# Loads, ones, masks and visits: four rearrangements in a fused attention and SwiGLU kernel on one core

## The chip, the cores and the metric

One core of a Trainium2 chip runs the whole kernel. The metric is device time in microseconds (us), the median of several executions of one build. Each execution also has its span (what the profile covers, some 1.7 to 1.9 us shorter) and the mean clock that the throttle granted TensorE. An execution that is over 1.5% above the fastest of the same kernel is called slow. Verdicts use the others and a threshold of 2%.

## The reference

Attention with ALiBi-like slopes over 8 global keys and the last 96 keys, then a feed-forward block. There are 4 batches, 8 heads, 768 positions and head size 64.

```python
rel = pos[:, None] - pos[None, :]
is_global = pos[None, :] < 8
is_local = (rel >= 0) & (rel < 96)
keep = is_global | is_local
dist = np.where(is_global & ~is_local, 96.0, np.abs(rel))
scores = q @ k.T / 8 - slopes * dist          # -1e9 where not keep, then softmax
x = (softmax @ v)                             # (3072, 512)
xn = x / sqrt(mean(x*x) + 1e-6) * rms_g
g = xn @ w_gate                               # 512 x 1536
out = (g * sigmoid(g) * (xn @ w_val)) @ w_out # 1536 x 512
```

## The kernel before

The positions are cut into 8 *units* of 384 (half a batch). A list scheduler with estimated durations puts every operation on an engine, in an order that is fixed when the kernel is built. Attention of a unit makes scores (`sc`), exps (`P`), a product with a table (`TB`, the exp of the bias with zeros for the mask), values (`avp`) and a norm; then *feed* `fc` does the feed-forward of one unit. TensorE is meant to be busy all the time: attention of later units is slipped between the matmuls of a feed. Unit 0 and feed 0 have nothing to slip into. Feed 0 runs in two parts, of one block and of two blocks of 128 positions ("part 1" below is the second).

The parts that matter here (cuts marked `...`):

```python
# the first block of unit 0: f32 by the SP queue, cast, small transposes
def load_first(name, g):
    nc.sync.dma_start(both[ds(64 * g, 64), "qk".index(name)], ...)
def cast_first(name, eng): ...            # both -> first, bf16
def tr_first(g):                          # 8 transposes of 64x64, twice
    ...
# the column of ones beside V, which gives the softmax's sum
def ones(i):
    nc.vector.memset(V1[i][:, :, :, 64:65], 1.0)
...
ones_ops = [add("DVE", 0.1, 0.15, 5.0 + 10 * i, ones, i) for i in range(2)]

# a visit to the scores: one head pair p, diagonal (d=0) or off-diagonal (d=1) blocks
def qk(c, p, d):
    sc = [bank([128, 512], F32, tag="sc", ...) for hh in range(2)]
    for i in range(HB):                   # HB = 3 blocks of 128
        ...
            nc.tensor.matmul(sc[hh][:, ts(i, 128)], k_of(...)[r], q_of(c, p, i)[r], ...)
def ex(c, p, d, hh):                      # exp of up to 384 columns
    nc.scalar.activation(T["P", c, p, d][:, hh, lo:HB, :], ...)
def mask(c, p, d, eng): ...
em = "POOL" if c == 1 and not d else "DVE"     # unit 1's diagonal masks on GpSimd
def table_copy():
    nc.gpsimd.tensor_copy(TB[:, :, 2], TB[:, :, 1])
# the small copy of the global keys that an off-diagonal visit of units 0 and 1 needs: kg, 128x16
# an order that matters later: every load waits for the one eight before it
more["deps"] = list(more.get("deps", ())) + loads[-8:-7]
```

The softmax here doesn't subtract the row's maximum and nothing guards it: scores larger than these inputs give would overflow.

Of the kernel before, what the change touches and what calls it, by code (L numbers as in the profile page):

```python
# [13 lines left out]
F32 = mybir.dt.float32  # L14
# [128 lines left out]
def kernel(  # L143
# [59 lines left out]
    both = mp.tile([128, 2, 4, 2 * D], F32, tag="h", name="both", bufs=2)  # L203

    def load_first(name, g):
        nc.sync.dma_start(both[ds(64 * g, 64), "qk".index(name)],
                          (q if name == "q" else k)[0, ds(4 * g, 4), 0:128].rearrange("h (p i) d -> p h (i d)", i=2))

# [15 lines left out]
    for g in range(2):  # L224
        for name in "qk":
            load_first(name, g)
# [28 lines left out]
    nc.vector.memset(VG[0][:, :, :, 64:65], 1.0)  # L255
    ts_, stt = nc.vector.tensor_scalar, nc.vector.scalar_tensor_tensor
# [35 lines left out]
    def ones(i):  # L292
        nc.vector.memset(V1[i][:, :, :, 64:65], 1.0)

    def table_copy():
        nc.gpsimd.tensor_copy(TB[:, :, 2], TB[:, :, 1])
# [28 lines left out]
    def cast_first(name, eng):  # L325
        if "first" not in T:
            T["first"] = mp.tile([128, 2, 2, 4, D], BF16, tag="t", name="first", bufs=3)
        n = "qk".index(name)
        (nc.scalar.copy if eng == "ACT" else nc.vector.tensor_copy)(
            T["first"][:, n].rearrange("p i h d -> p h i d"), both[:, n].rearrange("p h (i d) -> p h i d", i=2))  # L330

    def tr_first(g):
        t = bank([128, 2, 2, 128], BF16, tag="v", name="trf", bufs=2)
        r = slice(64 * g, 64 * g + 64)
        for n in range(2):
            for x in range(2):
                for i in range(2):
                    nc.tensor.transpose(t[:, n, x, ds(64 * i, 64)], T["first"][r, n, i, ds(2 * x, 2), :], ident[r, r])
        T["trf", g] = t

# [9 lines left out]

    def cp_first(g, name, eng):
        copy = nc.scalar.copy if eng == "ACT" else nc.vector.tensor_copy
        d = qT_tile(0)[:, 0, ds(2 * g, 2)] if name == "q" else slots(0)[:, 0, ds(2 * g, 2), 0:128]
        copy(d.rearrange("p h (t i) -> p h t i", i=2),
             T["trf", g][:, "qk".index(name)].rearrange("p h (i t) -> p h t i", i=2))
# [24 lines left out]
    def ex_block(i, d, hh):  # L380
        t = ptp.tile([128, 2, HB, 128], BF16, tag=f"P{hh}", name=f"P{hh}", bufs=4)
        T["Pb", i, d, hh] = t.rearrange("p h i t -> p (h i) t")[:, 0:HP]
        nc.scalar.activation(T["Pb", i, d, hh], T["sb", i, d][hh], AF.Exp, scale=float(scale))
# [145 lines left out]
    def qk(c, p, d):  # L529
        half = c % 2  # L530
        sc = [bank([128, 512], F32, tag="sc", name=f"sc{hh}", bufs=2) for hh in range(2)]
        for i in range(HB):
            J = HB * half + i - d
            if J < 0:
                continue
            cu, j = (c, i - d) if i - d >= 0 else (c - 1, HB - 1)
            for hh in range(2):
                r = slice(64 * hh, 64 * hh + 64)
                nc.tensor.matmul(sc[hh][:, ts(i, 128)], k_of(cu, p, j, NG * d)[r], q_of(c, p, i)[r],  # L539
                                 start=True, stop=True)  # L540
        T["sc", c, p, d] = sc

    def ex(c, p, d, hh):
        lo = 1 if (c % 2 == 0 and d) else 0
        if ("P", c, p, d) not in T:
            T["P", c, p, d] = ptp.tile([128, 2, HB, 128], BF16, tag=f"P{d}", name=f"P{d}", bufs=4)
        nc.scalar.activation(T["P", c, p, d][:, hh, lo:HB, :],  # L547
                             T["sc", c, p, d][hh][:, ds(128 * lo, CH - 128 * lo)], AF.Exp,
                             scale=float(scale))

    def mask(c, p, d, eng):
        half = c % 2
        mul = (nc.vector if eng == "DVE" else nc.gpsimd).tensor_tensor
        P = T["P", c, p, d]
        if d == 0:
            m = TB[:, ds(2 * p, 2), 0:HB] if half == 0 else _brd(TB[:, ds(2 * p, 2), 1], 2, HB)
            mul(P, P, m, op=ALU.mult)  # L557
        else:
            lo = 1 if half == 0 else 0
            mul(P[:, :, lo:HB, :], P[:, :, lo:HB, :], _brd(TB[:, ds(2 * p, 2), 3], 2, HB - lo), op=ALU.mult)  # L560

# [3 lines left out]
    def av(c, p):  # L565
        b, half = divmod(c, 2)
        P0, P1 = T["P", c, p, 0], T["P", c, p, 1]
        o = bank([128, HB, 2, 65], F32, tag=av_tag(c, p), name="avp", bufs=1)
        for i in range(HB):
            I = HB * half + i  # L570
            for hh in range(2):
                h = 2 * p + hh
                nc.tensor.matmul(o[:, i, hh, :], P0[:, hh, i, :], V1[b % 2][:, I, h, :],  # L573
                                 start=True, stop=(I == 0))
                if I > 0:
                    nc.tensor.matmul(o[:, i, hh, :], P1[:, hh, i, :], VG[b % 2][:, I - 1, h, :],  # L576
                                     start=False, stop=True)
# [45 lines left out]
    def xt_tile(fc):  # L623
        if ("xT", fc) not in T:
            T["xT", fc] = xp.tile([128, 4, CC, 128], BF16, tag="xT", name="xT", bufs=3)
# [53 lines left out]
    def fh(fc, f):  # L679
        n = 128 * FCH[fc][1]  # L680
        if ("h", fc) not in T:
            T["h", fc] = mp.tile([128, FC, 512], BF16, tag="h", name="hb", bufs=2)
# [25 lines left out]
    def fh0(lo, n, f0):  # L708
        if ("h", 0) not in T:
            T["h", 0] = mp.tile([128, FC, 512], BF16, tag="h", name="hb", bufs=2)  # L710
# [4 lines left out]
    OP = 3  # L715

# [32 lines left out]
    def store(fc, j):  # L749
# [3 lines left out]
        sizes=dict(g=2, v=2, o=1, sc=2, av=1, P0=4, P1=4, u=2, t=3, h=2, xT=3, xu=2, xn=2, ob=3,  # L753
# [33 lines left out]
    class _Landed:  # L787
        eng, dma, start = "SP", ("hw", 0.0), 0.0

        def __init__(self, t):  # L790
            self.done = t

    landed = {("q", 0): _Landed(4.2), ("k", 0): _Landed(4.5), ("q", 1): _Landed(4.8), ("k", 1): _Landed(5.2)}
    plan.sw = 3.0
    plan.rings["h"].append(_Buf("h", 0))
    plan.rings["t"].append(first_t := _Buf("t", 1))
# [30 lines left out]
    stage_buf = {c: {n: buf(n + "b", (HB - 1, HP, 1)[min(c, 2)]) for n in "qk"} for c in range(NU)}  # L827
# [5 lines left out]
    def attention0():  # L833
        ld, v_ops = loaded[0]
        for n, i, x in (("k", 1, 0), ("q", 1, 0), ("v", 0, 1), ("k", 2, 0), ("q", 2, 0), ("v", 1, 1), ("v", 2, 1)):
            if x:
                v_ops.append(load(load_v, (0, i, 1), 2.0, 0.84))
            else:
                ld[n, i] = load(load_qk, (0, n, i), 2.0, 0.84, take=[stage_buf[0][n]] if i == 1 else [])
        qT_buf[0], kT_buf[0] = buf("qT", 5), buf("kT", 5 + HP)  # L840
        cast = {n: add(e, *x, 4.0, cast_first, n, e, deps=[landed[n, 1]])
                for n, e, x in (("q", "DVE", (0.53, 0.6)), ("k", "ACT", act(512)))}
        ready = {}
        def copies(o, t, key, fn, n, due):
            ready[key] = []
            for name, e in (("q", "ACT"), ("k", "DVE")):
                take = [] if key != ("f", 0) else [qT_buf[0] if name == "q" else kT_buf[0]]
                ready[key].append(add(e, *(act(n) if e == "ACT" else dve(n)), due, fn, key[1], name, e, deps=[o],
                                      give=[t], take=take, after=ready["f", 0][-1:] if key != ("f", 0) and name == "k" else ()))
        for g in range(2):  # L850
            t = buf("v", 2)
            o = add("PE", 0.5, 0.75, 5.0, tr_first, g, deps=list(cast.values()), take=[t],
                    give=[first_t] if g else [])
            copies(o, t, ("f", g), cp_first, 256, 5.5)
        kgo = add("DVE", 0.15, 0.2, 6.5, kg_first, deps=[ready["f", 0][1], ready["f", 1][1]])
        kT_ready[0, "g"] = kgo
        for i in range(1, HB):
            t = buf("v", 2)
            o = add("PE", 0.7, 0.95, 7.0, tr_block, i, deps=[ld["q", i], ld["k", i]], take=[t],
                    give=[stage_buf[0]["q"], stage_buf[0]["k"]])  # L860
            copies(o, t, ("b", i), cp_block, 512, 6.5 + i)
        base = ready["f", 0] + ready["f", 1]
# [4 lines left out]
        for i in range(HB):  # L867
            due = (7.0, 9.6, 10.8)[i]
            ms = []
            for d in ((0,), (0, 1), (1, 0))[i]:  # L870
# [6 lines left out]
                for hh in range(2):  # L877
                    Pb = buf(f"P{hh}")
                    e = add("ACT", *act(512), due + 0.5, ex_block, i, d, hh, deps=[o], give=[bufs[hh]], take=[Pb])
                    ms.append((e, Pb))  # L880
# [3 lines left out]
                    deps=[m for m, _ in ms] + v_ops[:i + 1] + [ones_ops[0]] + ([vg_ev[i - 1]] if i else []),  # L884
                    take=ab, give=[b for _, b in ms])
# [6 lines left out]
        for lo, n in ((0, 1), (1, 2)):  # L892
# [10 lines left out]
            roots[lo - 1] = r  # L903
# [14 lines left out]
        front.extend([x_part[1], [o]])  # L918
# [7 lines left out]
    def attention(c):  # L926
# [7 lines left out]
        kT_buf[c] = buf("kT", 2 * HP if half == 0 else HP)  # L934
        qT_buf[c] = buf("qT", 2 * HP)
# [42 lines left out]
        for p in range(HP):  # L978
            a = a0 + step * p
            es = {}  # L980
            for d in range(2):
                bufs = [buf("sc"), buf("sc")]
                Pb = buf(f"P{d}")
# [214 lines left out]
```

## Time and profile before

| | before |
|---|---|
| time, median of 3 | 261.1 us (260.88 to 261.25) |
| first transposes on TensorE | 9.84 us |
| last exp of unit 0 ends | 20.73 us |
| first long gate matmul group of part 1 starts | 28.80 us |
| first gate matmul of feed 1 (the chain's; one other began at 62.98) | 63.43 us |
| last matmul ends | 256.35 us |

I cut the span at the last three of these: the *front* up to 28.80, *unit 1* from there to 63.43 (34.63 us), the *body* from there to the last matmul (192.92 us). The page of the kernel before, its first line of busy time (us, share of the span, instructions):

```profile
PE 242.7 (93%) x2013; PEld 139.3 (54%) x2013; DVE 175.9 (68%) x384; ACT 143.0 (55%) x347; POOL 86.5 (33%) x115
```

TensorE (PE) has 17 us of its span left in which it does nothing. The rest of the reading is in the prediction.

### The profile page before, as it was taken

The page shows a single profiled execution, that of the slowest core. Times are in us where ns is not written, and L with a number is a line of the kernel's source. Part 1 is how long each engine was busy: PE and PEld are TensorE (multiplying, and loading weights), DVE is VectorE, ACT ScalarE, POOL GpSimd, SP SyncE. Part 2 cuts the span into 40 slices and gives each one's busy share as a digit, 9 for nine tenths or more (in the row PEclk, how much of TensorE's full clock was granted, in tenths as well). Part 3 has the DMA queues.
Part 4 walks back from the last instruction along what each step waited for, and adds up shares of the span by engine and source line. Part 5 has one row for each costly group of instructions (what it writes and reads, how often), then busy time and mean ns, then how long its engine had stood idle before and what let it go on. Part 6 is the DMA issues. An engine that isn't in the chain of part 4 may idle for free.

```text
span 260.1 us, 5333 instructions
## 1 busy us (share of the span) xinstructions
PE 242.7 (93%) x2013; PEld 139.3 (54%) x2013; DVE 175.9 (68%) x384; ACT 143.0 (55%) x347; POOL 86.5 (33%) x115
## 2 busy tenths in 40 slices
PE   6496995999999889999999999999999999999994
PEld 5345583865555355555555555455545555565541
DVE  6456368863899469798758866876777776665520
ACT  4378795756666566655566464646375545243311
POOL 7557657369400850107510920175010001000000
PEclk9689599999999999999999999999999999999999
DMA  9999999999998799247995999399924011410113
GB/s 116 89 179 198 207 186 195 130 77 148 213 129 148 81 170 138 62 103 51 150 189 137 93 140 180 84 111 113 207 74 83 0 43 40 102 43 0 42 47 117
DMA packets 106212, 30.01 MB, mean 115 GB/s; under 512 B 96382, under 2 KB 102394, under 8 KB 106186
## 3 DMA queue, kind: packets, MB, share of 16 engines
q0 software_dynamic: 73392, 13.90, 67.8%
q1 hardware_dynamic: 32642, 15.63, 30.5%
q8 instruction: 16, 0.26, 0.4%
q10 hardware_dynamic: 152, 0.13, 0.1%
q14 instruction: 10, 0.08, 0.1%
HBM read 28.58 MB, written 6.29 MB: 134 GB/s over the span
## 4 chain that ended last, share of the span: by engine, by line
PE 87%; DVE 6%; ACT 3%; issue 2%; ACTq 0%; DVEq 0%
PE ops L728 24%; PE gps L656 22%; PE vps L656 21%; PE sc L539 5%; PE gp L690 3%; PE vp L690 3%; PE avp L573 2%; PE avp L576 2%; DVE kT L511 2%; PE sb L369 1%; PE sb L377 1%; PE trp L465 1%; ACT osb L733 1%; PE trb L345 1%; ACT xT L428 1%
## 5 line engine op out<-in xcount | busy, mean ns | idle before, releaser
L728 PE MATMUL ops<-w_out,hb 128*128 128x512 bf16 x288 | 71.5, 379 | 1.3 <-ACT osb L733 0.7
L669 ACT ACTIVATE t<-gps 128x384 f32<-128x384 f32 x84 | 41.0, 490 | 48.5 <-PE gps L656 46.5
L656 PE MATMUL vps<-xT,w_val 128*128 128x384 bf16 x336 | 66.5, 326 | 0.0
L656 PE MATMUL gps<-xT,w_gate 128*128 128x384 bf16 x336 | 65.7, 326 | 0.2
L547 ACT ACTIVATE P<-sc 128x384 bf16<-128x384 f32 (+1 forms) x112 | 46.3, 468 | 31.3 <-PE sc L539 31.1
L675 DVE SCALAR_TENSOR_TENSOR u<-t,gps 128x384 f32<-128x384 f32 x84 | 46.2, 552 | 25.2 <-ACT t L669 23.4
L683 DVE TENSOR_TENSOR hb<-u,vps 128x384 bf16<-128x384 f32 x84 | 45.3, 549 | 12.2 <-PE vps L656 11.5
L656 PEld LDWEIGHTS <-w_val 128*128 128x128 bf16 x336 | 31.1, 98 | 23.6
L728 PEld LDWEIGHTS <-hb 128*128 128x128 bf16 x288 | 27.4, 98 | 28.7 <-issue 1.5
L656 PEld LDWEIGHTS <-w_gate 128*128 128x128 bf16 x336 | 30.5, 98 | 21.5 <-issue 0.8
L608 POOL TENSOR_SCALAR m<-ssq 128x3 f32<-128x3 f32 x6 | 1.4, 232 | 73.8 <-ACT junk L596 73.8
L212 POOL DMA_DIRECT2D V<-in_v_dram x24 | 21.5, 931 | 3.6 <-DVE T L278 3.6
L539 PE MATMUL sc<-qT,kT 64*128 64x128 bf16 x312 | 19.1, 220 | 3.4 <-DVE kT L511 2.7
L733 ACT ACTIVATE osb<-ops 128x512 f32<-128x512 f32 x23 | 13.7, 594 | 14.4 <-PE ops L728 14.1
L458 POOL DMA_DIRECT2D kb<-in_k_dram x20 | 18.3, 924 | 4.7 <-DMA w_gate<-in_moe_w_gate_dram 1.8
L539 PEld LDWEIGHTS <-kT 64*128 64x128 bf16 x312 | 9.1, 94 | 19.9 <-issue 16.5
L596 ACT ACTIVATE junk<-xu 128x512 bf16<-128x512 bf16 (+1 forms) x29 | 15.6, 539 | 4.4 <-DVE xu L586 3.8
L458 POOL DMA_DIRECT2D qb<-in_q_dram x20 | 17.9, 916 | 0.2
L586 DVE TENSOR_TENSOR xu<-avp,rc 128x384 bf16<-128x384 f32 x28 | 15.6, 557 | 1.0
L560 DVE TENSOR_TENSOR P<-P,TB 128x768 bf16<-128x768 bf16 (+1 forms) x28 | 13.9, 498 | 3.5 <-ACT P L547 3.2
L557 DVE TENSOR_TENSOR P<-P,TB 128x768 bf16<-128x768 bf16 x24 | 13.3, 552 | 3.3 <-ACT P L547 3.2
L573 PE MATMUL avp<-V,P 128*128 128x65 bf16 x168 | 13.2, 193 | 0.0
(126 smaller groups left out, 240.6 us busy)
## 6 DMA issues: line engine op xcount, KB each, us to landing
out_dram<-osb SPq DMA_DIRECT2D x23, 256.0 KB, 2.0
V<-in_v_dram POOLq DMA_DIRECT2D x24, 128.0 KB, 6.6
kb<-in_k_dram POOLq DMA_DIRECT2D x20, 128.0 KB, 4.5
qb<-in_q_dram POOLq DMA_DIRECT2D x20, 128.0 KB, 5.1
w_gate<-in_moe_w_gate_dram POOLq DMA_DIRECT2D x3, 512.0 KB, 13.2
w_val<-in_moe_w_val_dram POOLq DMA_DIRECT2D x3, 512.0 KB, 15.0
w_out<-in_moe_w_out_dram POOLq DMA_DIRECT2D x3, 512.0 KB, 14.2
VG<-V SPq DMA_DIRECT2D x3, 365.6 KB, 4.5
```

The source lines that it names most:

```text
L212: nc.gpsimd.dma_start(V1[b % 2][:, HB * half + j, :, 0:D], v[b, :, ds(CH * half + 128 * j, 128)].rearrange("h p d -> p h d"))
L458: nc.gpsimd.dma_start(t[:, i], src[:, ds(128 * i, 128)].rearrange("h p d -> p h d"))
L539: nc.tensor.matmul(sc[hh][:, ts(i, 128)], k_of(cu, p, j, NG * d)[r], q_of(c, p, i)[r], start=True, stop=True)
L547: nc.scalar.activation(T["P", c, p, d][:, hh, lo:HB, :], T["sc", c, p, d][hh][:, ds(128 * lo, CH - 128 * lo)], AF.Exp, scale=float(scale))
L573: nc.tensor.matmul(o[:, i, hh, :], P0[:, hh, i, :], V1[b % 2][:, I, h, :], start=True, stop=(I == 0))
L656: nc.tensor.matmul(g[:, 0:128 * n], w[:, cc, ts(f, 128)], T["xT", fc][:, 0:n, cc, :], start=(cc == 0), stop=(cc == CC - 1))
L669: nc.scalar.activation(t[:, 0:n], T["g", fc, f][:, 0:n], AF.Tanh, scale=0.5)
L675: nc.vector.scalar_tensor_tensor(u[:, 0:n], T["t", fc, f][:, 0:n], 1.0, T["g", fc, f][:, 0:n], op0=ALU.add, op1=ALU.mult)
L683: nc.vector.tensor_tensor(T["h", fc][:, f, 0:n], T["u", fc, f][:, 0:n], T["v", fc, f][:, 0:n], op=ALU.mult)
L690: nc.tensor.matmul(g[:, x], w[:, cc, ts(f0 + x, 128)], T["xT", 0][:, ds(lo, n), cc, :], start=(cc == 0), stop=(cc == CC - 1))
L728: nc.tensor.matmul(o, T["h", fc][:, f, ts(j, 128)], w_out[:, f, :], start=(f == 0), stop=(f == FC - 1))
L733: nc.scalar.activation(t, T["o", fc, j], AF.Copy, scale=0.5)
```

## The change

The intent was to take away two long waits before feed 1 and to make fewer, fuller visits after it. (1) The ones are set before any load. (2) All of unit 0 comes by GpSimd's software loads in bf16, so that casts and small transposes go. (3) No mask and no table copy on GpSimd. (4) A unit's scores are visited in three visits for two head pairs instead of two for each pair, with up to 512 columns an exp. The core of the diff:

```diff
-    both = mp.tile([128, 2, 4, 2 * D], F32, tag="h", name="both", bufs=2)
-    def load_first(name, g): ...
-    for g in range(2):
-        for name in "qk":
-            load_first(name, g)
     nc.vector.memset(VG[0][:, :, :, 64:65], 1.0)
+    for i in range(2):
+        nc.vector.memset(V1[i][:, :, :, 64:65], 1.0)
...
-        nc.gpsimd.tensor_copy(TB[:, :, 2], TB[:, :, 1])
+        nc.scalar.copy(TB[:, :, 2], TB[:, :, 1])
-    def cast_first(name, eng): ...
-    def tr_first(g): ...
...
+    def visits(c, g):
+        lo = 1 - c % 2
+        every = [(2 * g + x, d, i) for d in range(2) for x in range(2) for i in range(d * lo, HB)]
+        cuts = (0, 4, 7, 10) if lo else (0, 4, 8, 12)
+        return [(cuts[k], every[cuts[k]:cuts[k + 1]]) for k in range(3)]
-    def qk(c, p, d):
+    def qk(c, g, k):
...
-        mul = (nc.vector if eng == "DVE" else nc.gpsimd).tensor_tensor
+        nc.vector.tensor_tensor(P, P, m, op=ALU.mult)
...
-        for n, i, x in (("k", 1, 0), ("q", 1, 0), ("v", 0, 1), ("k", 2, 0), ("q", 2, 0), ("v", 1, 1), ("v", 2, 1)):
+        for n, i, x in (("k", 0, 0), ("q", 0, 0), ("k", 1, 0), ("q", 1, 0), ("k", 2, 0), ("q", 2, 0), ("v", 0, 1), ("v", 1, 1), ("v", 2, 1)):
...
-                em = "POOL" if c == 1 and not d else "DVE"
-    ones_ops = [add("DVE", 0.1, 0.15, 5.0 + 10 * i, ones, i) for i in range(2)]
-    table_dup = [add("POOL", 1.0, 1.1, 40.0, table_copy, deps=table_ops)]
+    table_dup = [add("ACT", *act(1024), 44.0, table_copy, deps=table_ops)]
```

## The prediction

> **What bounds the kernel now.** I read the page first: TensorE is busy for 93% of the span, VectorE 68%, ScalarE 55%, GpSimd 33%, so any gain has to be time in which TensorE stands or runs slowly. Then the chain that ended last, in order of time (start us, length us, what):
>
> ```profile
> 5.40 3.58 issue
> 9.37 0.42 DVE first L329
> 9.84 0.82 PE trf L338 x14
> ...
> 40.04 3.91 DVE kT L511
> 43.94 0.05 issue
> 43.99 0.29 PE sc L539 x4
> ```
>
> Up to 63.4 us (the first gate matmul of feed 1) the chain leaves TensorE twice for long: 3.58 us from 5.40 and 3.91 us from 40.04. From 63.43 to 256.35 it is nearly all TensorE. The table of waits names both holes (us in total, times, longest):
>
> ```profile
> PEld L539 <- issue: 16.5, 51, 0.6
> ...
> PE trf L338 <- DVE first L329: 4.6, 1, 4.6
> ...
> DVE T L278 <- issue: 3.6, 1, 3.6
> POOL V L212 <- DVE T L278: 3.6, 1, 3.6
> ...
> PE sc L539 <- DVE kT L511: 2.7, 1, 2.7
> ```
>
> First hole. The timelines of VectorE and GpSimd show the ring. The memset of ones (L293) stands, in program order, behind the second of VectorE's four scaled tables, and as the V tile is tracked whole it waits for the first V load. That load was issued at 3.35 and landed 5.6 us later, at 8.95. GpSimd's next V load waits for the memset, so GpSimd stands still from 6.0 to 9.56 and the DMA queue drains (42 GB/s in 9 to 10 us, none in 10 to 11). The cast of the first queries stands behind the memset, so the first transposes start at 9.84.
>
> Second hole. A copy of 128x16 elements takes 3.90 us, while the same form takes 0.16 us at 35.08 and 0.17 us at 46.93:
>
> ```profile
> 40.04 3.90 DVE L511 COPY kT<-kT 128x16 bf16<-128x16 bf16 x1
> 40.66 3.23 POOL L557 TENSOR_TENSOR P<-P,TB 128x768 bf16<-128x768 bf16 x2
> ```
>
> The first line is from VectorE's timeline and the second from GpSimd's. The copy ends 0.05 us after the two masks on GpSimd. TensorE waits 2.74 us of it.
>
> The body. In the chain, four matmuls of 128x384 usually take 0.65 us, but 0.76 after a visit to the attention scores; the 0.27 us between two of these lines is such a visit:
>
> ```profile
> 107.81 1.30 PE vps L656 x8
> 109.38 0.76 PE gps L656 x4
> ```
>
> **What the Trainium skill says.** "TensorE: Matmul & The Clock Gate", Part 1: the clock is halved when TensorE has been idle for a free-running window of about 3.4 us and returns after a busy one. The trace agrees: the last filler ends near 5.2, the table of windows has the clock at 1.00 to 8 us, 0.88 in 8 to 9, then 0.50, and full again from about 15.6; a second half-speed stretch runs from about 25.9 to 32.6. "GPSIMD Engine Reference", Key points: GpSimd shares its SBUF interfaces with VectorE and contends with two-port VectorE instructions. The 3.90 us copy agrees. "DMA: Bandwidth & Descriptors", Issuing engines are not separate DMA queues: loads from different issuers interleave on the same 16 engines. The trace agrees: the first pair of keys on the SP queue landed in 3.2 us, the second, beside the software loads, in 5.2. "ScalarE: Activation LUTs", What ACT_TABLE_LOAD costs: an ACTIVATE has a fixed part of which about 93 ns overlaps with its neighbour. Here two of 384 columns take 0.87 us together, 0.435 each, so 0.32 for the columns (the page's 0.833 ns each) and some 0.11 fixed.
>
> **The change part by part.**
>
> *Ones ahead of the loads.* Two memsets of 0.10 us move to VectorE's start and the rest of its tables move back by about 0.2 us (the distance table is done at 4.95 instead of 4.77). The ring of waits is gone: GpSimd can issue nine loads, at 0.88 us each, back to back to about 9.5; the first weight load goes out then instead of at 11.29.
>
> *Unit 0 by software loads.* It removes four SP loads, two casts and sixteen small transposes, and adds eight transposes of 128x128 and one filler group. Landing: a load issued to an idle queue took 3.4 us (V at 9.56, queries at 52.65), the next one landed 1.9 us after it, later ones about 1.0 apart. Keys 0 then land near 4.9, queries 0 near 6.9, queries 1 near 8.9. TensorE's order puts four table matmuls first. They need all eight scaled tables: four on ScalarE at 0.45 us from 4.95, so 6.8. TensorE has idled only from 5.1 to 6.8, so by the window above I expect full clock there: 4 x 0.22 = 0.9 to 7.7 (0.45 a pair at 17.39), then eight transposes and nine fillers at 0.073 (0.44 for six at 34.71) to 8.9, second transposes from there to 9.5. With their copies the first score matmuls start near 10 instead of 12.48. After that ScalarE sets the pace: ten exps at 0.53, a query copy and a square are 6.5 us, with some 0.6 us of waits, against 7.7 us before. Its first exp moves from 13.05 to about 10.7, its last ends near 17.9 instead of 20.73. Part of that is given back: the transposes of the first normalized block now stand after the last attention matmuls and not before, and their four evictions (1.4 us, in turn on two engines) come later. I carry 2.1 us to the transposes of part 1 (25.78 before, 23.7 after). If the clock is halved there after all, it is 0.6.
>
> *No masks on GpSimd.* GpSimd loses four masks of 1.64 us and a copy of 1.05. VectorE gets four masks of about 0.55 (2.2 us, in a stretch where it is 54 to 80% busy), ScalarE the copy of 1024 columns (0.95 us). The 2.74 us wait goes. ScalarE was busy without a break from 28.3 to 41.8, so its extra 0.95 us could replace the wait; but unit 1 also loses four exp instructions (0.4 us), and walking the new order by hand I find scores and exps meeting within some tenths. At the end of unit 1 the new order puts all 36 output matmuls ahead of the 12 transposes for feed 1, where the old one hid the evictions behind the last eight. By hand the transposes wait 0.5 us for the norm and feed 1 waits 1.2 us for evictions; before, only the first gate group ran long (1.75 against 1.30). Net for 28.8 to 63.4: 2.74 + 0.3 (two visits fewer) - 1.7 + 0.45 = 1.8 us.
>
> *Three visits for two head pairs.* Scores go from 8 visits per unit to 6; exps from 112 to 84 (28 x 0.1 = 2.8 us of ScalarE, off the path). TensorE does the same matmuls. From feed 1 on their pure time, by the chain's best pieces, is 184.1 us: 672 x 0.1625 (0.65 for four), 252 x 0.216 (0.86 for four), 264 scores at 0.045 (0.27 for six), 264 value matmuls at 0.030 and some transposes. The chain took 192.9. The 8.8 us of excess over 48 visits is 0.18 us a visit, which fits 0.11 after a visit (0.76 against 0.65) and 0.06 to 0.1 before it. Twelve visits fewer: 2.1 us.
>
> Sum: 2.1 + 1.8 + 2.1 = 6.0 us. From the median of 261.1 that is 255.1; I add 0.2 for a wait not foreseen and say 255.3.
>
> **The rivals.** (a) *The front is hidden.* If weights set the start of feed 0, an earlier attention gains nothing. Against: no TensorE wait in the table names a weight load. For: the first value weights landed at 21.0 and were used at 22.8. Then the front gains about 0.5, and the time is 256.9. (b) *ScalarE becomes the bound in unit 1*: the copy and the wider exps put it behind and the 2.74 us return as TensorE waiting for exps: 258.0. For: it is 85 to 89% busy from 20 to 40 us. (c) *The clock stays full* from 25.9 to 32.6, because the gap before part 1 is shorter. The 5 us of matmuls at half speed from 28.8 would shrink by half: 252.8. For: the filler of 18 matmuls. Against: it stands ahead of the gap, not in it. (d) *Wider visits stall*: one visit uses both score banks, and the next must wait for two exps of 512 columns, 1.07 us. In the new order only about three visits after feed 1 come within 1.5 us of another, so at most 1 us is lost: 256.3.
>
> **Range and chances.** Three terms of about 2 us, each uncertain by 1.0 to 1.5, give a spread near 2 us: 252.7 to 257.8. Two per cent is 255.9, less than one us above my value, so faster has 0.60, same 0.39, and slower 0.01, as nothing adds TensorE work.
>
> **What would show it.** Right: VectorE without its 3.6 us idle after 5.4; first score matmul between 9.5 and 10.5; clock not halved at 6.8 us; no 128x16 copy above 0.3 us; no tensor masks on GpSimd; feed 1 starting near 59.2 instead of 63.4; and from there to the last matmul about 190.8 us instead of 192.9. Wrong: a first score matmul after 11.4 (cold clock), TensorE waiting for exps in 30 to 50 us, a feed 1 start after 61, or an unchanged 193 us from feed 1 on, which would say that the excess does not go by visits.

## The result, and the profile after

The changed kernel took 253.83 us (253.02 to 257.86, 4 executions), the kernel before 261.18 (260.88 to 263.71, 4). The ratio is 0.9684, 95% interval 0.9620 to 0.9749: faster. Ratios here are the mean of one kernel's fast executions over the mean of the other's in the same rounds, so not quite the ratio of the medians.

The execution that was profiled first was the 257.86 one, which is slow. So I ran the same text again, as the first run below: 254.18 us (253.75 to 254.92, 6 executions), ratio 0.9735 (0.9700 to 0.9770), profiled in a fast execution. Unless I say otherwise, "after" is that profile. The cuts:

| start or length, us | before | after, fast | after, slow |
|---|---|---|---|
| front ends (part 1's long gate group) | 28.80 | 25.13 | 27.89 |
| unit 1, to feed 1 | 34.63 | 32.28 | 33.06 |
| body, feed 1 to last matmul | 192.92 | 191.00 | 191.01 |
| span | 260.1 | 252.4 | 256.0 |

The three gains of the fast profile are 3.67, 2.35 and 1.92 us; with the 0.24 us longer tail they make the 7.7 us of the spans.

*The front.* TensorE's timeline of after (start us, us, instruction, and in brackets the idle time before it and what ended it):

```profile
6.61 1.02 PE L337 MATMUL sb<-T,ident 128*128 128x512 bf16 x4 [1.56 <-ACT T L273]
9.22 0.40 PE L345 MATMUL sb<-qT,kT 64*128 64x128 bf16 x8
22.62 0.66 PE L392 MATMUL xtb<-ident,xn 128*128 128x128 bf16 x8 [1.62 <-DVE xn L385]
25.13 2.95 PE L666 MATMUL gp<-xT,w_gate 128*128 128x256 bf16 x14 [0.51 <-ACT xT L398]
```

The four table matmuls come first and at full clock (0.22 us apart), the first scores are at 9.22 us instead of 12.41, and part 1's transposes at 22.62 instead of 25.78. The first of these lines in the slow execution:

```profile
6.60 1.86 PE L337 MATMUL sb<-T,ident 128*128 128x512 bf16 x4 [1.50 <-ACT T L273]
```

There the same four take 0.43 us each, so half clock, which lasted to about 16 us. The first scores come at 11.06 us.

What ends the front is new. The chain that ended last, after (start us, length us, what):

```profile
10.15 9.73 DMA w_val<-in_moe_w_val_dram
19.89 0.65 issue
20.54 0.88 POOL V L206
21.42 0.02 issue
21.44 0.75 POOL r L380
```

`r` is the root of part 1's norm, on GpSimd. Its input was ready at 19.82 us, but a load of V stood ahead of it in GpSimd's order, and that load waited for the load eight before it, the value weights. So in this profile the weights decide when the root can start. They also hold up TensorE once by name: the value matmuls of part 0 wait 0.52 us for them, to 19.93 us. In the slow profile the root waited for its sums instead (ready at 23.01 us, root at 23.10).

*Unit 1 and the body.* From the table of waits of after (us in total, times, longest):

```profile
PE sc L517 <- ACT P L526: 1.0, 3, 0.5
```

```profile
PEld L517 <- issue: 13.4, 39, 0.5
```

The 2.7 us wait for the small key copy is gone. The second line answers to the 16.5 us and 51 times of before: twelve times fewer and 3.1 us less. All four small copies of VectorE take 0.16 or 0.17 us in this profile (one took 0.57 us in the slow one).

### The profile page after: what moved, and what is told of

It reads as the page before. It is cut to its first block, busy times and chain, and to the rows that moved or that the text cites. A ratio compares the mean times of both kernels' runs of the same rounds, so it can differ in the third digit from the quotient of the medians.

```text
span 256.0 us, 5297 instructions
## 1 busy us (share of the span) xinstructions
PE 241.7 (94%) x2011; PEld 143.2 (56%) x2034; DVE 173.0 (68%) x386; ACT 139.4 (54%) x318; POOL 80.7 (32%) x112
## 4 chain that ended last, share of the span: by engine, by line
PE 86%; ACT 6%; DVE 5%; issue 1%; POOL 0%; POOLq 0%; ACTq 0%; DVEq 0%
PE gps L632 22%; PE ops L705 22%; PE vps L632 21%; PE sc L517 4%; PE gp L666 3%; PE vp L666 3%; PE avp L549 2%; PE avp L552 2%; ACT junk L572 1%; PE sb L337 1%; PE trb L319 1%; ACT P L526 1%; PE sb L345 1%; ACT T L273 1%; PE trp L435 1%
## 5 line engine op out<-in xcount | busy, mean ns | idle before, releaser
L645 ACT ACTIVATE t<-gps 128x384 f32<-128x384 f32 x84 | 40.9, 491 | 60.5 <-PE gps L632 59.2
L705 PE MATMUL ops<-w_out,hb 128*128 128x512 bf16 x266 | 68.6, 379 | 1.8 <-DVE xT L616 0.5
L526 ACT ACTIVATE P<-sc 128x512 bf16<-128x512 f32 (+1 forms) x84 | 43.0, 566 | 20.0 <-PE sc L517 20.0
L632 PEld LDWEIGHTS <-w_gate 128*128 128x128 bf16 x336 | 31.3, 98 | 21.7 <-issue 1.0
L536 DVE TENSOR_TENSOR P<-P,TB 128x768 bf16<-128x768 bf16 (+1 forms) x56 | 28.2, 525 | 10.4 <-ACT P L526 10.3
L428 POOL DMA_DIRECT2D kb<-in_k_dram x21 | 19.2, 920 | 4.6 <-DMA w_gate<-in_moe_w_gate_dram 1.8
L428 POOL DMA_DIRECT2D qb<-in_q_dram x21 | 18.7, 909 | 1.2 <-DMA w_out<-in_moe_w_out_dram 1.0
L517 PE MATMUL sc<-qT,kT 64*128 64x128 bf16 x312 | 16.4, 219 | 1.0 <-ACT P L526 1.0
L549 PEld LDWEIGHTS <-P 128*128 128x128 bf16 x168 | 11.8, 98 | 3.0
## 6 DMA issues: line engine op xcount, KB each, us to landing
out_dram<-osb SPq DMA_DIRECT2D x23, 256.0 KB, 2.1
```

The costliest lines, as they stand in the source:

```text
L428: nc.gpsimd.dma_start(t[:, i], src[:, ds(128 * i, 128)].rearrange("h p d -> p h d"))
L517: nc.tensor.matmul(sc[hh][:, ts(x, 128)], k_of(cu, p, j, NG * d)[r], q_of(c, p, i)[r], start=True, stop=True)
L526: nc.scalar.activation(T["P", c, g][:, hh, ds(s0, n)].rearrange("p s t -> p (s t)"), T["sc", c, g, k][hh][:, 0:128 * n], AF.Exp, scale=flo ...
L536: nc.vector.tensor_tensor(P, P, m, op=ALU.mult)
L549: nc.tensor.matmul(o[:, i, hh, :], P[:, hh, slot(c, p, 0, i)], V1[b % 2][:, I, h, :], start=True, stop=(I == 0))
L632: nc.tensor.matmul(g[:, 0:128 * n], w[:, cc, ts(f, 128)], T["xT", fc][:, 0:n, cc, :], start=(cc == 0), stop=(cc == CC - 1))
```

## The experiments

Twelve runs were made, two of them without an edit, and all were correct. "A" and "B" below are the theories of the expectation just above. The time "before" on the same chip: 261.39 us for the first four runs, 262.06 for the next four, 261.75 for the last four. The kernel before itself spread from 259.1 to 264.3 us.

| run | median us (range) | ratio to before | front ends | unit 1 | body |
|---|---|---|---|---|---|
| after_again | 254.18 (253.75 to 254.92) | 0.9735 | 25.13 | 32.28 | 191.0 |
| ones_early | 258.18 (257.34 to 258.96) | 0.9881 | 28.34 | 31.45 | 192.8 |
| masks_dve | 258.23 (257.32 to 259.87) | 0.9892 | 28.07 | 31.77 | 192.6 |
| visits_only | 257.24 (256.00 to 259.13) | 0.9872 | 28.77 | 30.67 | 191.0 |
| after_roots | 253.32 (251.85 to 256.11) | 0.9683 | 25.30 | 30.89 | 191.0 |
| after_fill_start | 254.19 (252.62 to 254.78) | 0.9715 | 26.51 | 31.37 | 191.0 |
| after_cold | 253.57 (253.06 to 257.71) | 0.9710 | 25.49 | 30.89 | 191.0 |
| after_pool_masks | 253.54 (252.45 to 255.48) | 0.9710 | 25.12 | 32.20 | 191.0 |
| sp_front | 256.82 (256.72 to 257.96) | 0.9827 | 29.12 | 32.34 | 191.0 |
| before_fill | 261.68 (260.69 to 261.95) | 1.0003 | 27.72 | 35.78 | 192.8 |
| roots_fill | 252.56 (251.93 to 253.40) | 0.9664 | 24.25 | 30.87 | 191.0 |
| before_again | 262.28 (one look) | | 29.06 | 34.72 | 193.0 |

The three columns on the right come from the one profiled execution of each, the medians from all. The intervals of the ratios reach 0.0035 to 0.0054 to either side.

**The changed kernel again**, no edit.

> The changed kernel again, for a profile in its fast state. Its one profile so far is a slow run of 256.0 us span at mean clock 0.984; its other runs had 251.2 to 252.4 us at 0.99 to 1.00. Theory A (clock): fast runs have no half-speed stretch between 26.9 and 32.7 us, and nothing else differs, so the span is 251.3 to 252.5, the first gate matmuls of part 1 take about 1.6 us for fourteen instead of 3.14, and feed 1 starts at 56.5 to 58.5 instead of 60.95. Theory B (other): the clock has the same two states in the kernel before, feed 1 starts near 61 in the fast runs too, and the 4 us are won somewhere after it.

A: 254.18 us and feed 1 at 57.41 us. But the second half-speed stretch was there, only shorter (the 14 gate matmuls took 2.95 us, and not 1.6), so A was right on the time and half wrong on the reason. The 3.5 us between the fast and the slow profile lie before feed 1: 2.76 in the front and 0.78 in unit 1.

**One part alone: the ones early.**

```diff
+    for i in range(2):
+        nc.vector.memset(V1[i][:, :, :, 64:65], 1.0)
-    ones_ops = [add("DVE", 0.1, 0.15, 5.0 + 10 * i, ones, i) for i in range(2)]
```

> The kernel before with the two memsets of ones moved ahead of the loads, nothing else. If the ring of waits (memset on the first V load, next V load on the memset) costs what the chain showed, VectorE's idle stretch of 3.6 us after 5.4 and GpSimd's of 3.56 us shrink, and the first transposes start when the last SP load lands, at about 8.8 instead of 9.84; time 259.5 to 260.5. Rival: the SP loads land at 8.06 at best and hide it, so less than 0.5 us is won, 260.6 or more.

More was won than expected, 3.1 us by the ratio (0.0119 of 261.4), and in another place: the first transposes came earlier, but the front ended only 0.46 us earlier. The gain is in unit 1, 34.63 to 31.45 us: the wait for the key copy had gone, though every mask and the table copy were still on GpSimd. VectorE's and then GpSimd's timeline:

```profile
39.32 0.46 DVE L513 COPY kT<-kT 128x16 bf16<-128x16 bf16 x1
```

```profile
38.72 1.04 POOL L298 COPY TB<-TB 128x1024 bf16<-128x1024 bf16 x1 [2.34 <-ACT TB L291]
39.72 3.24 POOL L559 TENSOR_TENSOR P<-P,TB 128x768 bf16<-128x768 bf16 x2
```

This is the row of the kernel before: the copy begins during the table copy, and two masks follow without a gap. Yet here the copy ended with the table copy (39.78 against 39.76 us) and did not wait for the masks. So such a row does not make the stall by itself. Which engine goes first at the end of a GpSimd instruction, and why, these runs do not show.

**One part alone: masks and table copy off GpSimd.**

```diff
-        nc.gpsimd.tensor_copy(TB[:, :, 2], TB[:, :, 1])
+        nc.scalar.copy(TB[:, :, 2], TB[:, :, 1])
-                em = "POOL" if c == 1 and not d else "DVE"
+                em = "DVE"
```

> The kernel before with the four masks of unit 1 on VectorE and the table copy on ScalarE, nothing else. Theory: the 3.9 us copy of 128x16 falls to 0.2 and TensorE's 2.74 us wait goes, so 258.3 to 259.0. Rival: ScalarE, with no break from 28 to 42 us and 0.95 us more to do, becomes the bound there and less than 1 us is won, 260 or more.

As expected: 258.23 us, unit 1 shorter by 2.86 us, the stall gone. One key copy still took 0.56 us (from 38.90), with nothing on GpSimd but the issue of a load (38.62 to 39.49): it ended with that issue.

**One part alone: the visits.** The hunks of `visits`, `qk`, `ex`, `mask`, `av` and the attention loop, with unit 1's diagonal masks left on GpSimd.

> The kernel before with the three visits for two head pairs alone (old front, masks of unit 1 still on GpSimd). Theory (0.18 us of excess per visit, 14 visits fewer): feed 1 to the last matmul takes about 191 us instead of 192.9, and the time is 258.5 to 259.5. Rival: the excess goes by matmuls and not by visits, and the time stays within 0.5 us of 261.1.

The body shrank from 192.9 to 191.0 us, as expected of visits. But the time fell by 3.3 us by the ratio (0.0128 of 261.4), because the stall shrank here too. VectorE's and then GpSimd's timeline of this run:

```profile
35.48 0.80 DVE L513 COPY kT<-kT 128x16 bf16<-128x16 bf16 x1
37.98 0.81 DVE L513 COPY kT<-kT 128x16 bf16<-128x16 bf16 x1
```

```profile
35.21 1.04 POOL L296 COPY TB<-TB 128x1024 bf16<-128x1024 bf16 x1 [3.22 <-ACT TB L289]
37.09 1.66 POOL L568 TENSOR_TENSOR P<-P,TB 128x768 bf16<-128x768 bf16 x1
```

Each copy ends with the GpSimd instruction that ran when it began (36.28 against 36.25 us, 38.79 against 38.75). It is held up for 0.6 us only, although the issue of a load follows at once on GpSimd (at 36.19 and 38.68 us). This profile also had no second half-speed stretch (14 gate matmuls in 1.69 us); it was the fastest of its six executions.

So each of three parts alone removes the same 2.7 us. Their single gains (3.1, 2.8 and 3.3 us, together 9.2) are more than the whole change won (6.9 and 8.3 us by its two ratios), and part (2) is not among them: the stall can be removed only once.

**The changed kernel with one part undone: masks and table copy back on GpSimd.**

```diff
-        nc.scalar.copy(TB[:, :, 2], TB[:, :, 1])
+        nc.gpsimd.tensor_copy(TB[:, :, 2], TB[:, :, 1])
+                        em = "POOL" if c == 1 and not d else "DVE"
```

> The changed kernel with one part undone: the four masks of unit 1 on the diagonal blocks and the table copy are back on GpSimd. Theory A (the masks on GpSimd as such held the small key copy of VectorE, and taking them away won the 2.7 us): one copy of 128x16 takes over 2 us again, from part 1 to feed 1 34 us instead of 32.3, 255.5 to 256.8 us. Theory B (the stall needs a copy that begins while masks stand back to back on GpSimd, a matter of the order, and the new order of visits has none): copies of 0.2 to 0.9 us, no wait of TensorE over 0.5 us for one, 253.2 to 254.8 us.

B: 253.54 us, nothing lost. GpSimd's and VectorE's timeline:

```profile
34.22 1.64 POOL L536 TENSOR_TENSOR P<-P,TB 128x768 bf16<-128x768 bf16 x1 [1.42 <-ACT P L526]
36.76 1.65 POOL L536 TENSOR_TENSOR P<-P,TB 128x768 bf16<-128x768 bf16 x1
```

```profile
32.98 0.17 DVE L481 COPY kT<-kT 128x16 bf16<-128x16 bf16 x1
35.71 0.18 DVE L481 COPY kT<-kT 128x16 bf16<-128x16 bf16 x1
```

The masks come one at a time, with loads or idle time between them, and these two copies fall at an end of a mask or in idle time (the other two took 0.17 and 0.26 us). In the whole change, part (3) is worth nothing measurable.

**The changed kernel with one part undone: SP loads for the first block.** The text of visits_only with the ones early and the masks off GpSimd.

```diff
-        for n, i, x in (("k", 0, 0), ("q", 0, 0), ("k", 1, 0), ...
+        for n, i, x in (("k", 1, 0), ("q", 1, 0), ("v", 0, 1), ...
+    for g in range(2):
+        for name in "qk":
+            load_first(name, g)       # with casts and small transposes, as before
```

> The changed kernel with one part undone: the first block of unit 0 comes again by SP loads in f32, with two casts and sixteen small transposes; the ones stay early, the masks off GpSimd, the visits three for two pairs. Theory A (the software loads, with the table matmuls first on TensorE, are most of the front's gain; the ones alone moved part 1's first gate matmul only from 28.80 to 28.34): that matmul near 28 us, feed 1 near 59 to 59.5, 256.3 to 258.0 us. Theory B (the ring of waits at the ones was the front's cost, the loads' road matters little): that matmul near 25.5, 254.0 to 255.5 us.

A: 256.82 us, and the front ended at 29.12, no earlier than before. TensorE's timeline:

```profile
9.52 0.62 PE L340 MATMUL trf<-ident,first 64*128 64x64 bf16 x12 [1.76 <-ACT first L331]
11.89 0.61 PE L379 MATMUL sb<-qT,kT 64*128 64x128 bf16 x8
```

The first scores come at 11.89 us, against 9.22, and at half clock. So part (2), with the order on TensorE that comes with it, makes the front's gain, and not part (1): about 2.6 us by the medians (from different calls), 0.9 to 1.4% by the ratios. A part of it goes with the clock: in the slow profile of after, half clock lasted about as long in the front (to 15.86 us, here to 15.61), and that front ended only 1.23 us earlier than this one (27.89 and 29.12).

**The clock at the start.** One run with 14 more fillers before the table matmuls, one with none.

```diff
     def mk_block(i, d):
+        if (i, d) == (0, 0):
+            idle_n[0] += 14            # after_fill_start; after_cold: idle_n[0] = 0, also in rms_tr
```

> The changed kernel with 14 more filler matmuls ahead of the first table matmuls, so that TensorE is not idle from 5.1 to 6.6 us. Theory A (the slow and the fast executions of the changed kernel differ in whether the clock was halved in that idle time, by the phase of its window): no slow execution any more, the four table matmuls always take about 1.0 us, and the time is that of the fast ones, 253.5 to 254.5 us, with a spread under 1.2 us. Theory B (the states have another cause): one or two of six executions at 256 us or more, as before.

> The changed kernel without the fillers ahead of the first work, so that TensorE does nothing before 6.6 us but one small transpose and starts at half clock: the four table matmuls at 0.43 us each, 1.7 us. Theory A (the front's gain hangs on the clock): part 1's first gate matmul near 27.5 to 28.5 us, feed 1 near 60.5, 256.5 to 258.0 us, about the one slow execution seen (257.9). Theory B (the gain is the earlier landing of the loads, whatever the clock): 254.0 to 255.3 us.

A fails in after_cold, and after_fill_start does not bear it out. Without fillers the start is cold for certain, and yet five of six executions are fast. Two lines of its TensorE timeline:

```profile
6.61 1.87 PE L340 MATMUL sb<-T,ident 128*128 128x512 bf16 x4 [2.92 <-ACT T L273]
25.49 1.69 PE L669 MATMUL gp<-xT,w_gate 128*128 128x256 bf16 x14 [0.52 <-ACT xT L401]
```

The first scores are 1.25 us later than in the fast profile of after (10.47 against 9.22), but the front ends only 0.36 us later: the root waits for the weights' load either way (GpSimd waited for it until 20.89 us, against 20.54). And the clock is full in part 1. With more fillers there was no slow execution in six, as A wanted, but also none in the six of after_again, and the spread was 2.2 us instead of under 1.2. Its profile, with full clock from the first table matmul to 21.27 us, adds to the case against the weights: they landed at 20.90 us instead of 19.89, the root started at 22.45 instead of 21.44, and the front ended at 26.51 instead of 25.13 (half clock from 21.27 us on has a share in the last). That the start's half-speed stretch must end soon for a fast execution fits the profiles of the changed kernel and its variants (it ended near 9 us in after_cold and near 16 in the slow one), but only one slow execution was profiled. In every trace the recorded changes of the clock lie whole steps of 3.41 us apart, and the steps lie elsewhere in each execution (the last section shows two): full clock is recorded from 4.89 us in after, from 9.41 in after_cold, from 15.86 in the slow one. So where the steps fall is a likely cause of the states. What decides in which step the start's stretch ends, these runs don't settle.

**The root ahead of the load.** The chain of after says that GpSimd's V load holds the root.

```diff
-    loads[-1].after.append(roots[0])
+    for x in loads[-2:]:
+        x.after.append(roots[0])
```

> The changed kernel with one order changed: GpSimd takes the root of the second part's norm ahead of the V load that it otherwise waits 2.0 us for (it stood at 20.54 to 21.42 us, in front of the root, while its sums had been ready at 19.82). Theory A (in the undisturbed state that root is what ends the front): the root ends near 20.6 instead of 22.2, part 1's first gate matmul starts near 23.6 instead of 25.1, and as the gap on TensorE is then under 2 us the clock may stay full and the 14 matmuls take 1.7 us and not 2.95; 251.3 to 252.8 us. Theory B (weights or evictions end the front anyway): 253.8 to 254.4 us, unchanged.

Unclear. 253.32 us is less than 1 us better, within the intervals, and the profiled execution had a cold start, so its root could not start before 20.77 us:

```profile
20.77 0.73 POOL L380 TENSOR_TENSOR r<-m,half_c 128x2 f32<-128x2 f32 x1 [1.74 <-DVE m L375]
```

It did start as soon as its sums were there (VectorE's `m`, 20.52 us), which is what the edit was for; the front gained 0.2 us against after_cold (25.30 and 25.49), which started as cold. One of the six executions was slow.

**The kernel before with fillers in its gap.**

```diff
     def xtr_part(lo, n):
+        if lo:
+            f = ps.tile([128, 128], F32, tag="o", name="fill", bufs=1)
+            for _ in range(20):
+                nc.tensor.matmul(f, zero, zero, start=True, stop=True)
     def fgv0(lo, n, f0, w, tag):
+        if lo and f0 == 0 and tag == "g":
+            idle_n[0] = 8
```

> The kernel before with 20 filler matmuls ahead of part 1's transposes and 8 ahead of its first gate matmul, where TensorE is idle for 1.9 us. Theory A (part of the gap between the kernels is the half-speed stretch from 25.9 to 32.6 us, which the changed kernel has shorter or not at all): the 14 gate matmuls of part 1 take 1.7 us instead of 3.15, feed 1 near 61.5, 259.0 to 260.5 us, and the executions of 263 to 264 us become rare. Theory B (what is won there is lost at the wait for the key copy in unit 1, where TensorE waits anyway): the 14 matmuls are faster but feed 1 stays near 63, 260.8 to 262.0 us.

B, and clearly: the ratio is 1.0003. TensorE's, VectorE's and GpSimd's timelines:

```profile
27.72 1.69 PE L696 MATMUL gp<-xT,w_gate 128*128 128x256 bf16 x14 [0.51 <-ACT xT L432]
```

```profile
41.07 5.11 DVE L515 COPY kT<-kT 128x16 bf16<-128x16 bf16 x1 [0.95 <-PE sc L543]
```

```profile
40.33 1.05 POOL L296 COPY TB<-TB 128x1024 bf16<-128x1024 bf16 x1
41.33 4.82 POOL L561 TENSOR_TENSOR P<-P,TB 128x768 bf16<-128x768 bf16 x3
```

The clock was full and the front ended 1.08 us earlier, and the 14 matmuls took 1.46 us less. But feed 1 started at 63.50 us, as before. GpSimd's table copy and the masks behind it began no earlier (40.33 us), now three masks stood in a row, and the copy waited out the table copy and all three: 5.11 us. What the front gained in this run, the stall took back.

**Both on the changed kernel**: the root first, 14 and 8 fillers in the gap.

> The changed kernel with the root of part 1 ahead of the V loads on GpSimd and with 14 filler matmuls ahead of part 1's transposes and 8 ahead of its first gate matmul. Theory A (the spread of the changed kernel's fast executions is the second half-speed stretch): the 14 gate matmuls always take 1.7 us, all clocks at 0.99 or more, 251.8 to 253.2 us and a spread under 1.5 us. Theory B (the fillers stand in the way, or the clock is lost in the first 16 us instead): 253.3 to 254.5 us with a spread of 2 us or more.

A: 252.56 us, all six executions within 1.5 us, all clocks at 0.999 or 1.0. GpSimd's and TensorE's timelines:

```profile
19.71 0.72 POOL L380 TENSOR_TENSOR r<-m,half_c 128x2 f32<-128x2 f32 x1 [1.61 <-DVE m L375]
```

```profile
24.25 1.69 PE L672 MATMUL gp<-xT,w_gate 128*128 128x256 bf16 x14 [0.52 <-ACT xT L402]
```

The root starts 1.73 us earlier than in after, the front ends 0.88 us earlier, and unit 1 is 1.41 us shorter. This is the best version. Its ratio to before is 0.9664 (0.9623 to 0.9705), that of after 0.9735 and 0.9684 in two sets. The two ran in different calls, so the gain of about 1.5 us over after is likely but not measured directly.

**The kernel before again**, no edit.

> The kernel before, unchanged, for a second profile of it. If the stall at the small key copy belongs to its order, one copy of 128x16 takes 2 us or more again, near 40 us, and TensorE waits over 2 us for it; if it was a chance of that execution, all four copies stay under 1 us and feed 1 starts near 60.5 instead of 63.4.

The stall came again, so it was not a chance of one execution. VectorE's timeline, and the table of waits:

```profile
40.31 3.97 DVE L511 COPY kT<-kT 128x16 bf16<-128x16 bf16 x1
```

```profile
PE sc L539 <- DVE kT L511: 2.8, 1, 2.8
```

## Why the prediction was right

It said 255.3 us, 252.7 to 257.8, and faster at 0.60. The fast result of 253.8 to 254.2 us is in the range, 1.1 to 1.5 us below the centre. By its own steps:

- *The front, predicted 2.1 us to part 1's transposes: measured 3.16 (25.78 to 22.62).* The mechanism was right: VectorE's 3.6 us of idle time after 5.4 us gone (it now waits 2.2 us from 6.5 on, for the transposes), nine loads back to back, first weights at 9.41 us, full clock at the table matmuls. The term was too small. The first exp came at 9.80 us instead of the predicted 10.7, and the ten exps with what lies between took 6.6 us instead of 7.2, so the last one ended at 16.42 and not 17.9. Of these 1.5 us more, 0.4 were lost again by a wait that the prediction didn't have: the root behind a V load behind the value weights.
- *Rival (a), the front hidden by weights: half true.* I had looked for a TensorE wait that names a weight load and found none. In after there is one, of 0.52 us. But what ended the front came by GpSimd's order, where a root stands behind a load that waits for weights. after_cold shows its size: 1.25 us more or less at the first scores moved the front's end by 0.36.
- *The clock, "0.6 if halved": near.* In the slow profile the front gained 0.91 us at its end. The reason given for full clock at the table matmuls (TensorE idle only from 5.1 to 6.8 us) did not hold in every execution: in the slow one the idle time was no longer (1.50 us against 1.56), and the table matmuls ran at half clock.
- *Unit 1, predicted 1.8 us: measured 2.35,* of which 0.2 us are the gate matmuls (2.95 against 3.15). The wait of 2.7 us went and about 0.6 us were given back. masks_dve, without the new order at the end of unit 1, gained 2.86.
- *But the reason for unit 1 was wrong.* The step "No masks on GpSimd: the 2.74 us wait goes" names one sufficient cause as the cause. ones_early and visits_only removed the wait with the masks still on GpSimd, and after_pool_masks put them back at no cost. In all three profiles with a stall of 3.9 us or more, a key copy began during the table copy, and two or three masks followed on GpSimd without a gap. That is not enough: ones_early has the same row and no stall. That each part breaks the stall by moving a copy or the row is argued and not shown.
- *Its signs.* The first scores (9.22 us, said 9.5 to 10.5) and feed 1 (57.41, said near 59.2) came earlier than it said; the other signs came true in the fast profile.
- *The body, predicted 2.1 us for twelve visits at 0.18: measured 1.9, so 0.16 a visit.* Right. It is the same in all nine profiles with the new visits (191.0) against 192.6 to 193.0 without, whatever the clock did in the front.
- *Rival (c), full clock in part 1:* it happens in some executions, and is worth 1.26 us by these lines (2.95 against 1.69), and 1.4 us in unit 1 as a whole (32.28 against 30.87). It fits the spread of the fast executions: with the gap filled (roots_fill) the clock was full in all six. *Rival (b)* and *(d)* stayed at 1.0 us of TensorE waits for exps together.
- *The sum* treated the terms as independent. For the whole change this did no harm, since the stall is removed once. That much is luck: the unit 1 term was credited to the masks, and the other parts would have brought it without them. For the parts the sum would have failed: three parts alone each won about 3 us.

## What to carry to other kernels

A wait between two engines that arises where two instructions happen to meet can go for more than one reason: here three parts each removed it alone. Ask of such a gain whether another part of the same change would have removed it already, and undo the part in the changed kernel, not only do it alone in the old one. And where an engine takes its work strictly in order, look at what stands in front of a short instruction on the critical path: a load issue that waits for weights can make the weights' landing the end of the front, though the matmuls that wait for them by name lose only 0.5 us, as in after.

## What the Trainium skill lacked or had wrong

- "SBUF — State Buffer", SBUF: two separate sides, says that of VectorE and GpSimd the one that starts first has the shared port pair for its whole instruction and the other blocks. It does not say which goes next when GpSimd's instructions follow one another without a gap. Here VectorE's copy was blocked for more than one: 3.90 and 3.97 us behind a table copy (1.05 us) and two masks, and 5.11 us behind a table copy and three masks. In ones_early, with the same table copy and two masks without a gap, it was held up for 0.46 us only, to the end of the table copy.
- "TensorE: Matmul & The Clock Gate", Part 1, gives an idle window of some 3.4 us as what halves the clock. In after no idle stretch was near that long: the clock fell at 25.37 us, and the idle stretches of TensorE just before were 1.62 and about 0.5 us; the same gaps in after_cold did not lower it. So partly filled windows count. The page does say that frequent short idles can make the clock swing, but no page says from which share on. In the 14 profiles, of the steps of 3.41 us at full clock up to the last matmul, the clock fell after all 11 in which TensorE was busy for up to 43%, after 4 of the 7 with 45 to 50%, and after none with 51% or more. The step before the fall in after and the one behind it (us, then busy us of TensorE first, the granted clock third from the right):

```profile
21.96:25.37 3.41, 1.71 (x15) 1.06 (x16) 1.82 (x5) 2.41 (x8) 2.25 (x4) 1.00 1.27 207
25.37:28.78 3.41, 3.41 (x22) 2.61 (x20) 0.71 (x2) 2.62 (x7) 2.26 (x5) 0.50 1.24 207
```

- No page says that the granted clock of a profile can read 1.00 before its first recorded change. In the slow execution it reads so from 6.6 to 16 us, where matmuls of 128x512 take 0.43 us each, twice the 0.22 of the fast one; and after_cold, which started as slowly, has a mean clock of 1.0. Durations decide.
